# Four edits at the seams of a TensorE-bound kernel: weight rows and first tile in order of arrival, fold copies swapped between two engines, attention ahead of three output tiles, one output half moved to another engine

## Chip, cores and metric

One core of a Trainium2 chip. The metric is the device time of one execution in microseconds (us). Before the change: 220.64 us, median of 3 runs (220.44 to 220.81). Engines are called as the profile calls them: PE is TensorE, PEld its weight loads, DVE VectorE, ACT ScalarE, POOL GpSimd, SP the engine that here only starts DMAs. PE writes its results to banks of PSUM, from which DVE or ACT copies them before a bank is used again (here the first k tile waits 0.74 us for such a copy). The granted clock is the share of PE's full clock in the profile's records.

## The reference, cut to what matters

```python
def _A_ref(x, wqkv, w_phi, wo):          # linear attention, 32 heads of 16
    q, k, v = split(x @ wqkv)
    pq, pk = q @ w_phi, k @ w_phi        # per head
    phi = concat(softmax(p), softmax(-p))
    kv, z = phi_k^T v, sum(phi_k)
    return (phi_q kv / phi_q z) @ wo
def _B_ref(x, w_in, w_sp, b_sp, w_out):  # gated MLP, 688 + 688 columns
    z = gelu(x @ w_in); z1 = z[:688]; z2 = layernorm(z[688:])
    return (z1 * (w_sp @ z2 + b_sp)) @ w_out
out = g * A + (1 - g) * B                # g = sigmoid(x . gate_w), x is 2048 x 512
```

The kernel multiplies w_phi into wq and wk once ("folds"), so that pq and pk are single products with x.

## The kernel before

It has three stages: A, z tiles (z2 = second half of w_in, z1 = first half), with the folds between them; B, k, v and q tiles with exps and the kv sums; C, the product with w_sp ("gg"), attention tiles and output tiles. Cuts are marked `...`. `warm_up(n)` issues n matmuls on constants whose result nobody reads; they are called fillers below.

```python
def load_z2w(eng, j, h):                 # four pieces: column half j, d rows 2h and 2h+1
    eng.dma_start(out=w_z2[:, 2*h:2*h+2, j*HF:(j+1)*HF],
                  in_=w_in_v[:, 2*h:2*h+2, FH+j*HF:FH+(j+1)*HF])
nc.sync.dma_start(out=xs[:, 0, :], in_=x2[0:P, :])
load_z2w(nc.scalar, 0, 0); load_z2w(nc.sync, 0, 1); load_z2w(nc.scalar, 1, 0)
nc.sync.dma_start(out=xs[:, 1, :], in_=x2[P:2*P, :])
load_z2w(nc.sync, 1, 1)
nc.scalar.dma_start(out=xs[:, 2:4, :], ...)
...
def fold(qk, dt):
    ...                                  # four 128-column matmuls into one bank, fps
    if dt % 2 == 0: nc.scalar.copy(out=dst[:, dt, :], in_=fps[:, :])
    else:           nc.vector.tensor_copy(out=dst[:, dt, :], in_=fps[:, :])

warm_up(7); x_T(0); warm_up(5, P)        # x_T: transpose one x tile on PE
z_half(zps[0], 0, w_z2, 0, HF, lambda: x_T(1))   # tile 0, half 0; x tile 1 in the middle
gate_T(); warm_up(2, P)
z_half(zps[1], 1, w_z2, 0, HF); warm_up(2, P)
z_half(zps[0], 0, w_z2, 1, HF + 1); z2_tile(0, zps[0])
z_half(zps[1], 1, w_z2, 1, HF + 1, lambda: x_T(2)); z2_tile(1, zps[1])
x_T(3); z2_tile(2); z2_tile(3); b_T()    # b_T: one small transpose, used as a mark below
...
for hh in range(1, 2 * NT):              # stage C
    tt, j = divmod(hh, 2); gg_half(tt, j)
    if j == 1: uTs[tt] = u_T(tt)
    if j == 1 and tt >= 2: ba_tile(tt - 2, ...)          # output tile
    for k in attn_at.get(hh, ()): oTs[k] = attn_tile(k)  # tiles 0-4 at odd hh, 5-9 at even
ba_tile(NT - 2, ...); ba_tile(NT - 1, ..., nsplit=2)     # each half: ACT scales, ACT's queue stores
```

The softmax here doesn't subtract the row's maximum and nothing guards it: scores larger than these inputs give would overflow.

Of the kernel before, what the change touches and what calls it, by code (L numbers as in the profile page):

```python
# [7 lines left out]
AF = mybir.ActivationFunctionType  # L8
ALU = mybir.AluOpType
AX = mybir.AxisListType  # L10
FP32 = mybir.dt.float32
BF16 = mybir.dt.bfloat16
I32 = mybir.dt.int32

P = 128
# [4 lines left out]
F = 1376  # L20
FH = 688
HF = FH // 2
NT = S // P
NDT = D // P
CH = 512
# [9 lines left out]
def kernel(  # L35
# [14 lines left out]
    nc = tc.nc  # L50
    x2 = A_x.flatten_outer_dims()
    out2 = out.flatten_outer_dims()
# [5 lines left out]
    psF = psF_cm.__enter__()  # L58

    xT = pers.tile([P, NDT, S], BF16, name="xT")  # L60
    w_z1 = early.tile([P, NDT, FH], BF16, name="w_z1")
    w_z2 = early.tile([P, NDT, WP], BF16, name="w_z2")
# [24 lines left out]
    g_inv = pers.tile([P, NT], FP32, name="g_inv")  # L87
# [9 lines left out]
    w_in_v = B_w_in.rearrange("(dt p) f -> p dt f", p=P)  # L97
# [6 lines left out]
        out=ramp[:, 0, :], data0=ones32[:, :], data1=zeros[:, :], initial=0.0,  # L104
        op0=ALU.add, op1=ALU.add,
# [6 lines left out]
            out=ident[qs, qs], in0=ramp[qs, 0, :], in1=ramp[qs, 1, :], op=ALU.is_equal)  # L112
    nc.gpsimd.dma_start(out=gaterow[:, :], in_=gate_w.rearrange("(dt p) -> dt p", p=P))
    nc.gpsimd.dma_start(out=brow[:, :], in_=B_b_sp.rearrange("(t p) -> t p", p=P))
    def load_z2w(eng, j, h):
        eng.dma_start(
            out=w_z2[:, 2 * h:2 * h + 2, j * HF:(j + 1) * HF],
            in_=w_in_v[:, 2 * h:2 * h + 2, FH + j * HF:FH + (j + 1) * HF])

    nc.sync.dma_start(out=xs[:, 0, :], in_=x2[0:P, :])  # L120
    load_z2w(nc.scalar, 0, 0)
    load_z2w(nc.sync, 0, 1)
    load_z2w(nc.scalar, 1, 0)
    nc.sync.dma_start(out=xs[:, 1, :], in_=x2[P:2 * P, :])
    load_z2w(nc.sync, 1, 1)
    nc.scalar.dma_start(
        out=xs[:, 2:4, :], in_=x2[2 * P:4 * P, :].rearrange("(i p) d -> p i d", p=P))
    for h in range(2):
# [60 lines left out]
    psA_cm = tc.tile_pool(name="psA", bufs=3, space=bass.MemoryType.PSUM, reuse_waits="tile")  # L189
    psA = psA_cm.__enter__()  # L190

    def z_half(zp, tt, wt, j, n, mid=None):
        for dt in range(NDT):
            if dt == 2 and mid is not None:
                mid()
            nc.tensor.matmul(  # L196
                zp[:, j, 0:n], lhsT=xT[:, dt, tt * P:(tt + 1) * P],
                rhs=wt[:, dt, j * HF:j * HF + n],
                start=(dt == 0), stop=(dt == NDT - 1),
            )  # L200

    def z_mm(tt, wt, w):
        zp = psA.tile([P, 2, CH], FP32, name="zp")
        for dt in range(NDT):
            for j in range(2):
                n = HF if j == 0 else w - HF
                nc.tensor.matmul(  # L207
                    zp[:, j, 0:n], lhsT=xT[:, dt, tt * P:(tt + 1) * P],
                    rhs=wt[:, dt, j * HF:j * HF + n],
                    start=(dt == 0), stop=(dt == NDT - 1),  # L210
                )
        return zp

    def z2_tile(tt, zp=None):
        if zp is None:
            zp = z_mm(tt, w_z2, FH + 1)
        z2v = z2all[:, tt, :].rearrange("p (j n) -> p j n", j=2)
        nc.scalar.activation(out=z2v, in_=zp[:, :, 0:HF], func=AF.Gelu_apprx_tanh)  # L218
        nc.vector.tensor_copy(out=glog[:, tt:tt + 1], in_=zp[:, 1, HF:HF + 1])
        for j in range(2):  # L220
            nc.vector.bn_stats(out=bn6[:, tt, j, :], in_=z2v[:, j, :])  # L221
        nc.vector.bn_aggr(out=mv[:, tt, :], in_=bn6[:, tt, :, :].rearrange("p j s -> p (j s)"))
# [18 lines left out]
                op0=ALU.subtract, op1=ALU.mult,  # L241
            )

    wp = psF.tile([P, CH], FP32, name="wp", tag="pq", bufs=2)

    def warm_up(n, w=CH):
        for _ in range(n):
            nc.tensor.matmul(
                wp[:, 0:w], lhsT=nc.const_aps.tensor(1.0, [P, P], BF16),
                rhs=nc.const_aps.tensor(1.0, [P, w], BF16), start=True, stop=True)  # L250

    def x_T(i):
        tp = psF.tile([P, NDT, P], BF16, name="tp", tag="pq", bufs=2)
        for dt in range(NDT):
            nc.tensor.transpose(tp[:, dt, :], xs[:, i, dt * P:(dt + 1) * P], ident[:, :])
        with tc.high_priority():
            nc.vector.tensor_copy(out=xT[:, :, i * P:(i + 1) * P], in_=tp[:, :, :])  # L257

    def gate_T():
        gt = psF.tile([P, NDT], BF16, name="gt", tag="pq", bufs=2)  # L260
        nc.tensor.transpose(gt[:, :], gaterow[:, :], ident[0:NDT, 0:NDT])
        for dt in range(NDT):
            nc.vector.tensor_copy(out=w_z2[:, dt, FH:FH + 1], in_=gt[:, dt:dt + 1])
# [19 lines left out]
    def fold(qk, dt):  # L283
        dst = wq_p if qk == 0 else wk_p
        fps = psF.tile([P, CH], FP32, name="fps", tag="pq", bufs=2)
        for kc in range(NDT):
            nc.tensor.matmul(
                fps[:, kc * P:(kc + 1) * P],
                lhsT=wqkT[:, qk * 4 + kc, dt * P:(dt + 1) * P],
                rhs=wphi[:, kc, :],  # L290
                start=True, stop=True,
            )
        if dt % 2 == 0:
            nc.scalar.copy(out=dst[:, dt, :], in_=fps[:, :])
        else:
            nc.vector.tensor_copy(out=dst[:, dt, :], in_=fps[:, :])  # L296

    with tc.manual_schedule(engines={mybir.EngineType.PE, mybir.EngineType.Activation}):
        warm_up(7)
        x_T(0)  # L300
        warm_up(5, P)
        zps = [psA.tile([P, 2, CH], FP32, name="zp") for _ in range(2)]
        z_half(zps[0], 0, w_z2, 0, HF, lambda: x_T(1))
        gate_T()
        warm_up(2, P)
        z_half(zps[1], 1, w_z2, 0, HF)
        warm_up(2, P)
        z_half(zps[0], 0, w_z2, 1, HF + 1)
        z2_tile(0, zps[0])
        z_half(zps[1], 1, w_z2, 1, HF + 1, lambda: x_T(2))  # L310
        z2_tile(1, zps[1])
        x_T(3)
        z2_tile(2)
        z2_tile(3)
        b_T()
        for c in range(NCH):
            ts = list(range(c * 4, c * 4 + 4))
            for tt in ts:
                if c > 0:
                    z2_tile(tt)  # L320
                if c >= 2 and tt % 2 == 0:
                    fold(3 - c, (tt % 4) // 2)
            for tt in ts:
                z1_tile(tt)
                if c >= 2 and tt % 2 == 0:
                    fold(3 - c, 2 + (tt % 4) // 2)
            z2_norm(ts)
            if c == 1:
                wphi_fold()
# [144 lines left out]
    def ba_tile(tt, uT, oT, nsplit=1):  # L474
        w = D // nsplit
        for h in range(nsplit):
            acc = mm_tile()
            ba_mm(acc[:, 0:w], uT, oT, h * w, (h + 1) * w)
            ob = work.tile([P, w], BF16, name=f"ob{nsplit}")
            nc.scalar.activation(out=ob[:, :], in_=acc[:, 0:w], func=AF.Copy, scale=g_inv[:, tt:tt + 1])  # L480
            nc.scalar.dma_start(out=out2[tt * P:(tt + 1) * P, h * w:(h + 1) * w], in_=ob[:, :])

    oTs = {}
    uTs = {}
    with tc.manual_schedule(engines={mybir.EngineType.PE, mybir.EngineType.Activation}):
        ks = {0: k_tile(0)}
        kvacc = [psM.tile([P, NG, 256], FP32, name=f"kvacc{a}", tag="kvat", bufs=2) for a in range(2)]
        pend = []
        for tt in range(NT):
            if tt + 1 < NT:  # L490
                ks[tt + 1] = k_tile(tt + 1)
            ek, rk = ks.pop(tt)
            pend.append((tt, ek, v_tile(tt, rk)))
            pq_tile(tt // 4, tt % 4)
            if len(pend) > 2:
                kv_acc(*pend.pop(0))
        nc.scalar.activation(out=g_el[:, :], in_=glog[:, :], func=AF.Exp)
        nc.vector.tensor_scalar(out=g_1p[:, :], in0=g_el[:, :], scalar1=1.0, scalar2=None, op0=ALU.add)
        nc.vector.reciprocal(out=g_inv[:, :], in_=g_1p[:, :])
        kv_acc(*pend.pop(0))  # L500
        gg_half(0, 0)
        kv_acc(*pend.pop(0))
        kvz_evac()
        work_cm.__exit__(None, None, None)
        work = ctx.enter_context(tc.tile_pool(name="workC", bufs=2, reuse_waits="tile"))
        attn_at = {}
        for tt in range(NT):
            attn_at.setdefault(2 * tt + (1 if tt < 5 else 0 if tt < 10 else -1), []).append(tt)
        for hh in range(1, 2 * NT):
            tt, j = divmod(hh, 2)  # L510
            gg_half(tt, j)
            if j == 1:
                uTs[tt] = u_T(tt)
            if j == 1 and tt >= 2:
                ba_tile(tt - 2, uTs.pop(tt - 2), oTs.pop(tt - 2))
            for k in attn_at.get(hh, ()):
                oTs[k] = attn_tile(k)
        ba_tile(NT - 2, uTs.pop(NT - 2), oTs.pop(NT - 2))
        ba_tile(NT - 1, uTs.pop(NT - 1), oTs.pop(NT - 1), nsplit=2)


# [28 lines left out]
```

## Time and profile before

| reading | value | view |
|---|---|---|
| time | 220.64 us | median of 3 runs |
| PE busy | 211.7 of 219.0 us | page, part 1 |
| second x tile transposed from | 6.30 us | PE timeline |
| small bias transpose (end of the z2 tiles 0 to 3) | 12.36 us | PE timeline |
| first k tile | 48.30 us | timeline |

Head of the page before: the engine's busy time, share of the span and instructions.

```profile
span 219.0 us, 3717 instructions
## 1 busy us (share of the span) xinstructions
PE 211.7 (97%) x1436; PEld 130.6 (60%) x1456; DVE 148.8 (68%) x381; ACT 74.0 (34%) x120; POOL 13.8 (6%) x51
```

Only PE is near its span, and the change looks for its gain in PE's waits. The list of PE's waits before, beside 0.8 us at the launch (us in total, times, longest):

```profile
PE mm L346 <- DVE wq_p L296: 0.7, 1, 0.7
PE tp L255 <- DMA xs<-in_A_x_dram: 0.6, 1, 0.6
PE mm L363 <- ACT eq_686 L396: 0.3, 1, 0.3
PE gt L261 <- DVE xT L257: 0.2, 1, 0.2
PE at_1685 L431 <- DVE m L451: 0.2, 1, 0.2
```

There are five waits of 2 us in all, and they are what the change aims at. The PE timeline of the front (start, duration, line, output<-inputs, shape, count, idle time before):

```profile
4.92 0.75 PE L196 MATMUL zp<-w_z_66,xT 128*128 128x344 bf16 x2
6.30 0.40 PE L255 MATMUL tp<-ident,xs 128*128 128x128 bf16 x4 [0.63 <-DMA xs<-in_A_x_dram]
6.53 0.46 PE L196 MATMUL zp<-w_z_66,xT 128*128 128x344 bf16 x2
7.21 0.16 PE L261 MATMUL gt<-ident,gaterow 4*128 4x4 bf16 x1 [0.23 <-DVE xT L257]
...
9.91 2.51 PE L207 MATMUL zp<-w_z_66,xT 128*128 128x344 bf16 x16
12.36 0.18 PE L267 MATMUL bt<-ident,brow 16*128 16x16 bf16 x1
```

PE waits for the second x tile at 6.30 and has no gap after the third z2 tile at 9.91. The seam between stages A and B, in the timeline of all engines:

```profile
46.09 1.56 DVE L238 TENSOR_SCALAR z2all<-z2all,mv,rstd 128x688 bf16<-128x688 bf16 x4 [1.46 <-POOL rstd L236]
46.23 1.33 PE L207 MATMUL zp<-w_z_65,xT 128*128 128x344 bf16 x8
47.57 0.68 DVE L296 CAST wq_p<-fps 128x512 bf16<-128x512 f32 x1
48.30 1.02 PE L346 MATMUL mm<-wk_p,xT 128*128 128x512 bf16 x3 [0.74 <-DVE wq_p L296]
48.35 1.28 ACT L350 ACT_TABLE_LOAD   x1
```

The last fold's copy stands behind four norms on DVE, and the first k tile needs that bank. The attention tile that waits, in the PE timeline of stage C:

```profile
130.09 2.50 PE L415 MATMUL mm<-z2all,wspT 128*128 128x344 bf16 x16
132.56 0.42 PE L431 MATMUL at_1684<-kvz,eq_685 128*128 128x144 bf16 x4
133.16 0.42 PE L431 MATMUL at_1685<-kvz,eq_686 128*128 128x144 bf16 x4 [0.17 <-DVE m L451]
133.42 2.50 PE L415 MATMUL mm<-z2all,wspT 128*128 128x344 bf16 x16
```

### The profile page before, as it was taken

The page shows a single profiled execution, that of the slowest core. Times are in us where ns is not written, and L with a number is a line of the kernel's source. Part 1 is how long each engine was busy: PE and PEld are TensorE (multiplying, and loading weights), DVE is VectorE, ACT ScalarE, POOL GpSimd, SP SyncE. Part 2 cuts the span into 40 slices and gives each one's busy share as a digit, 9 for nine tenths or more (in the row PEclk, how much of TensorE's full clock was granted, in tenths as well). Part 3 has the DMA queues.
Part 4 walks back from the last instruction along what each step waited for, and adds up shares of the span by engine and source line. Part 5 has one row for each costly group of instructions (what it writes and reads, how often), then busy time and mean ns, then how long its engine had stood idle before and what let it go on. Part 6 is the DMA issues. An engine that isn't in the chain of part 4 may idle for free.

```text
span 219.0 us, 3717 instructions
## 1 busy us (share of the span) xinstructions
PE 211.7 (97%) x1436; PEld 130.6 (60%) x1456; DVE 148.8 (68%) x381; ACT 74.0 (34%) x120; POOL 13.8 (6%) x51
## 2 busy tenths in 40 slices
PE   8899999989999999999999999999999999999993
PEld 3566666754455555567756665656666666666653
DVE  3376776757999999985867659547648576458610
ACT  2256666678776767650001110110011001100112
POOL 7120202020000000000000000000000000000000
PEclk9999999999999999999999999999999999999998
DMA  6999999999940000000332331331343314312331
GB/s 193 258 215 198 247 260 210 251 266 265 192 148 0 3 0 0 3 3 0 63 63 57 87 61 47 84 63 38 71 87 61 77 40 77 84 36 59 77 84 49
DMA packets 71890, 22.30 MB, mean 102 GB/s; under 512 B 65936, under 2 KB 71872, under 8 KB 71872
## 3 DMA queue, kind: packets, MB, share of 16 engines
q1 hardware_dynamic: 68016, 19.33, 43.1%
q10 hardware_dynamic: 3792, 2.73, 4.2%
q8 instruction: 11, 0.18, 0.4%
q14 instruction: 7, 0.06, 0.1%
q0 software_dynamic: 64, 0.01, 0.0%
HBM read 3.71 MB, written 2.10 MB: 27 GB/s over the span
## 4 chain that ended last, share of the span: by engine, by line
PE 89%; DVE 4%; DMA 2%; ACT 2%; issue 1%; POOL 1%; SPq 0%
PE mm L415 33%; PE zp L207 13%; PE mm L472 9%; PE mm L363 6%; PE mm L391 6%; PE mm L470 6%; PE mm L346 6%; DMA xs<-in_A_x_dram 2%; PE kvacc_707 L381 2%; PE kvacc_708 L381 2%; DVE bn_83 L221 1%; PE zp L196 1%; DVE z2all L238 1%; DVE wq_p L296 1%; ACT eq_685 L396 1%
## 5 line engine op out<-in xcount | busy, mean ns | idle before, releaser
L415 PE MATMUL mm<-z2all,wspT 128*128 128x344 bf16 x512 | 78.3, 309 | 0.0
L415 PEld LDWEIGHTS <-wspT 128*128 128x128 bf16 x512 | 49.5, 98 | 23.4
L207 PEld LDWEIGHTS <-xT 128*128 128x128 bf16 x240 | 22.9, 98 | 10.8 <-DVE xT L257 0.2
L472 PE MATMUL mm<-w_out_t,uT 128*128 128x512 bf16 (+1 forms) x102 | 23.5, 366 | 0.0
L369 DVE TENSOR_TENSOR vr<-mm,rk 128x512 bf16<-128x512 f32 x32 | 21.2, 668 | 1.0 <-PE mm L363 0.9
L352 DVE TENSOR_REDUCE zk<-ek 128x64 f32<-128x1024 bf16 x16 | 19.3, 1211 | 3.4 <-ACT ek L350 3.4
L207 PE MATMUL zp<-w_z_65,xT 128*128 128x344 bf16 x128 | 20.0, 309 | 0.0
L350 ACT ACTIVATE ek<-mm 128x512 bf16<-128x512 f32 x32 | 17.3, 598 | 3.0 <-PE mm L346 2.8
L207 PE MATMUL zp<-w_z_66,xT 128*128 128x344 bf16 x112 | 17.7, 310 | 0.0
L363 PE MATMUL mm<-wv_sb,xT 128*128 128x512 bf16 x64 | 16.4, 379 | 0.4 <-ACT eq_686 L396 0.3
L346 PE MATMUL mm<-wk_p,xT 128*128 128x512 bf16 x60 | 15.9, 379 | 0.9 <-DVE wq_p L296 0.7
L470 PE MATMUL mm<-wo_t,oT 128*128 128x512 bf16 (+1 forms) x54 | 15.7, 363 | 0.7
L472 PEld LDWEIGHTS <-uT 128*128 128x128 bf16 x102 | 10.0, 98 | 10.8
L391 PE MATMUL mm<-xT,wq_p 128*128 128x512 bf16 x62 | 16.0, 379 | 0.0
L218 ACT ACTIVATE z2all<-zp 128x688 bf16<-128x688 f32 x16 | 11.9, 743 | 11.6 <-PE zp L207 6.7
L221 DVE BATCH_NORM_STATS2 bn_83<-z2all 128x6 f32<-128x344 bf16 x32 | 14.9, 502 | 0.0
L226 ACT ACTIVATE z1all<-zp 128x688 bf16<-128x688 f32 x16 | 11.9, 743 | 6.9 <-PE zp L207 6.9
L420 DVE SCALAR_TENSOR_TENSOR ucat_92<-mm,bT,z1all 128x344 bf16<-128x344 f32 x12 | 6.9, 572 | 9.9 <-PE mm L415 9.9
L396 ACT ACTIVATE eq_685<-mm 128x512 bf16<-128x512 f32 x16 | 9.6, 597 | 10.6 <-PE mm L391 9.3
L458 DVE TENSOR_TENSOR o<-m 128x512 bf16<-128x512 f32 x16 | 10.9, 680 | 0.0
L363 PEld LDWEIGHTS <-xT 128*128 128x128 bf16 x64 | 6.2, 98 | 7.8 <-issue 0.6
L391 PEld LDWEIGHTS <-wq_p 128*128 128x128 bf16 x64 | 6.3, 98 | 7.6
(221 smaller groups left out, 207.8 us busy)
## 6 DMA issues: line engine op xcount, KB each, us to landing
w_z_65<-in_B_w_in_dram SPq DMA_DIRECT2D x2, 344.0 KB, 5.2
w_out_t<-in_B_w_out_dram SPq DMA_DIRECT2D x1, 640.0 KB, 5.3
wv_sb<-in_A_wqkv_dram SPq DMA_DIRECT2D x1, 512.0 KB, 4.6
wo_t<-in_A_wo_dram SPq DMA_DIRECT2D x1, 512.0 KB, 5.7
w_z_66<-in_B_w_in_dram ACTq DMA_DIRECT2D x2, 172.0 KB, 3.3
w_z_66<-in_B_w_in_dram SPq DMA_DIRECT2D x2, 172.0 KB, 4.3
xs<-in_A_x_dram SPq DMA_DIRECT2D x2, 128.0 KB, 3.5
xs<-in_A_x_dram ACTq DMA_DIRECT2D x1, 256.0 KB, 5.3
```

The costliest lines, as they stand in the source:

```text
L207: nc.tensor.matmul(zp[:, j, 0:n], lhsT=xT[:, dt, tt * P:(tt + 1) * P], rhs=wt[:, dt, j * HF:j * HF + n], start=(dt == 0), stop=(dt == NDT ...
L218: nc.scalar.activation(out=z2v, in_=zp[:, :, 0:HF], func=AF.Gelu_apprx_tanh)
L221: nc.vector.bn_stats(out=bn6[:, tt, j, :], in_=z2v[:, j, :])
L346: nc.tensor.matmul(k_ps[:, :], lhsT=xT[:, dt, tt * P:(tt + 1) * P], rhs=wk_p[:, dt, :], start=(dt == 0), stop=(dt == NDT - 1))
L350: nc.scalar.activation(out=ek[:, a, :], in_=k_ps[:, :], func=AF.Exp, scale=1.0 - 2.0 * a)
L352: nc.vector.tensor_reduce(out=zk[:, :], in_=ek[:].rearrange("p a (h e) -> p (a h) e", e=DH), axis=AX.X, op=ALU.add,)
L363: nc.tensor.matmul(v_ps[:, :], lhsT=xT[:, dt, tt * P:(tt + 1) * P], rhs=wv_sb[:, dt, :], start=(dt == 0), stop=(dt == NDT - 1))
L369: nc.vector.tensor_tensor(out=vr[:, a, :, 0:P].rearrange("p g (h d) -> p g h d", d=DH), in0=v_ps[:, :].rearrange("p (g h d) -> p g h d", g ...
L391: nc.tensor.matmul(pq[:, :], lhsT=wq_p[:, dt, g * P:(g + 1) * P], rhs=xT[:, dt, c0:c0 + CH], start=(dt == 0), stop=(dt == NDT - 1),)
L415: nc.tensor.matmul(gp[:, 0:HF], lhsT=wspT[:, st, tt * P:(tt + 1) * P], rhs=z2all[:, st, j * HF:(j + 1) * HF], start=(st == 0), stop=(st == ...
L470: nc.tensor.matmul(acc, lhsT=oT[:, g, :], rhs=wo_t[:, g, c0:c1], start=(g == 0), stop=False)
L472: nc.tensor.matmul(acc, lhsT=uT[:, ft, :], rhs=w_out_t[:, ft, c0:c1], start=False, stop=(ft == NFT - 1))
```

## The change

Its intent: start the first tile with the rows that are there, take the last fold away from the busy DVE (the edit swaps the two engines for all eight folds), give DVE more time between two attention tiles, and free the tail from ACT. The diff, cut to its core and partly put in words:

```diff
-    load_z2w(nc.scalar, 0, 0) ... (nc.sync, 0, 1) ... (nc.scalar, 1, 0) ... (nc.sync, 1, 1)
+    def load_z2w(eng, dt):
+        eng.dma_start(out=w_z2[:, dt, 0:FH], in_=w_in_v[:, dt, FH:F])
+    load_z2w(nc.scalar, 0) ... (nc.sync, 1) ... (nc.scalar, 2) ... (nc.sync, 3)
 ...
-        z_half(...) gate_T() warm_up(2, P) z_half(...) ...      # as printed above
+        z2_tile(0, order=[(0,0),(1,0),(2,0),(0,1),(1,1),(2,1),(3,0),(3,1)],   # (d row, half)
+                mid={(2,0): [gate_T, lambda: x_T(1)], (2,1): [lambda: warm_up(4, P)]})
+        z2_tile(1, mid={(1,1): [lambda: x_T(2)], (2,1): [lambda: x_T(3)]})
 ...
-        if dt % 2 == 0:          # fold: ACT copies the even d blocks
+        if dt % 2 == 1:          # the last fold is dt = 3
 ...
-            ACT scales both halves of the last tile, ACT's queue stores them
+            if h == 0: as before
+            else: nc.vector.tensor_scalar(out=ob, in0=acc, scalar1=g_inv, op0=mult); nc.sync.dma_start(...)
 ...
-            if j == 1 and tt >= 2: ba_tile(tt - 2, ...)   # always ahead of attention
+            tt >= 5: ahead of attn_tile as before; tt = 2, 3, 4: after attn_tile
```

The warm-up matmuls also move from a bank of the transposes to a bank of the z tiles.

More of the change, by code (lines that the diff above doesn't have):

```diff
@@ L114 @@
     nc.gpsimd.dma_start(out=brow[:, :], in_=B_b_sp.rearrange("(t p) -> t p", p=P))
-    def load_z2w(eng, j, h):
-        eng.dma_start(
-            out=w_z2[:, 2 * h:2 * h + 2, j * HF:(j + 1) * HF],
-            in_=w_in_v[:, 2 * h:2 * h + 2, FH + j * HF:FH + (j + 1) * HF])
+    def load_z2w(eng, dt):
+        eng.dma_start(out=w_z2[:, dt, 0:FH], in_=w_in_v[:, dt, FH:F])
     nc.sync.dma_start(out=xs[:, 0, :], in_=x2[0:P, :])
-    load_z2w(nc.scalar, 0, 0)
-    load_z2w(nc.sync, 0, 1)
-    load_z2w(nc.scalar, 1, 0)
+    load_z2w(nc.scalar, 0)
+    load_z2w(nc.sync, 1)
+    load_z2w(nc.scalar, 2)
     nc.sync.dma_start(out=xs[:, 1, :], in_=x2[P:2 * P, :])
-    load_z2w(nc.sync, 1, 1)
+    load_z2w(nc.sync, 3)
     nc.scalar.dma_start(
@@ L190, with z_mm @@
     psA = psA_cm.__enter__()
-    def z_half(zp, tt, wt, j, n, mid=None):
-        for dt in range(NDT):
-            if dt == 2 and mid is not None:
-                mid()
+    def z_mm(tt, wt, w, order=None, mid={}):
+        zp = psA.tile([P, 2, CH], FP32, name="zp")
+        for dt, j in order or [(dt, j) for dt in range(NDT) for j in range(2)]:
+            n = HF if j == 0 else w - HF
             nc.tensor.matmul(
@@ L200, in z_half, with z2_tile @@
             )
-    def z_mm(tt, wt, w):
-        zp = psA.tile([P, 2, CH], FP32, name="zp")
-        for dt in range(NDT):
-            for j in range(2):
-                n = HF if j == 0 else w - HF
-                nc.tensor.matmul(
-                    zp[:, j, 0:n], lhsT=xT[:, dt, tt * P:(tt + 1) * P],
-                    rhs=wt[:, dt, j * HF:j * HF + n],
-                    start=(dt == 0), stop=(dt == NDT - 1),
-                )
-        return zp
-    def z2_tile(tt, zp=None):
-        if zp is None:
-            zp = z_mm(tt, w_z2, FH + 1)
+            for f in mid.get((dt, j), ()):
+                f()
+        return zp
+    def z2_tile(tt, **kw):
+        zp = z_mm(tt, w_z2, FH + 1, **kw)
         z2v = z2all[:, tt, :].rearrange("p (j n) -> p j n", j=2)
@@ L242, in z2_norm @@
             )
-    wp = psF.tile([P, CH], FP32, name="wp", tag="pq", bufs=2)
+    wp = psA.tile([P, 2, CH], FP32, name="zp")
     def warm_up(n, w=CH):
@@ L248, in warm_up @@
             nc.tensor.matmul(
-                wp[:, 0:w], lhsT=nc.const_aps.tensor(1.0, [P, P], BF16),
+                wp[:, 0, 0:w], lhsT=nc.const_aps.tensor(1.0, [P, P], BF16),
                 rhs=nc.const_aps.tensor(1.0, [P, w], BF16), start=True, stop=True)
@@ L301 @@
         warm_up(5, P)
-        zps = [psA.tile([P, 2, CH], FP32, name="zp") for _ in range(2)]
-        z_half(zps[0], 0, w_z2, 0, HF, lambda: x_T(1))
-        gate_T()
-        warm_up(2, P)
-        z_half(zps[1], 1, w_z2, 0, HF)
-        warm_up(2, P)
-        z_half(zps[0], 0, w_z2, 1, HF + 1)
-        z2_tile(0, zps[0])
-        z_half(zps[1], 1, w_z2, 1, HF + 1, lambda: x_T(2))
-        z2_tile(1, zps[1])
-        x_T(3)
+        z2_tile(
+            0, order=[(0, 0), (1, 0), (2, 0), (0, 1), (1, 1), (2, 1), (3, 0), (3, 1)],
+            mid={(2, 0): [gate_T, lambda: x_T(1)], (2, 1): [lambda: warm_up(4, P)]},
+        )
+        z2_tile(1, mid={(1, 1): [lambda: x_T(2)], (2, 1): [lambda: x_T(3)]})
         z2_tile(2)
@@ L479, in ba_tile @@
             ob = work.tile([P, w], BF16, name=f"ob{nsplit}")
-            nc.scalar.activation(out=ob[:, :], in_=acc[:, 0:w], func=AF.Copy, scale=g_inv[:, tt:tt + 1])
-            nc.scalar.dma_start(out=out2[tt * P:(tt + 1) * P, h * w:(h + 1) * w], in_=ob[:, :])
+            dst = out2[tt * P:(tt + 1) * P, h * w:(h + 1) * w]
+            if h == 0:
+                nc.scalar.activation(out=ob[:, :], in_=acc[:, 0:w], func=AF.Copy, scale=g_inv[:, tt:tt + 1])
+                nc.scalar.dma_start(out=dst, in_=ob[:, :])
+            else:
+                nc.vector.tensor_scalar(
+                    out=ob[:, :], in0=acc[:, 0:w], scalar1=g_inv[:, tt:tt + 1], scalar2=None, op0=ALU.mult)
+                nc.sync.dma_start(out=dst, in_=ob[:, :])
     oTs = {}
@@ L513 @@
                 uTs[tt] = u_T(tt)
-            if j == 1 and tt >= 2:
+            ba = j == 1 and tt >= 2
+            if ba and tt >= 5:
                 ba_tile(tt - 2, uTs.pop(tt - 2), oTs.pop(tt - 2))
@@ L517 @@
                 oTs[k] = attn_tile(k)
+            if ba and tt < 5:
+                ba_tile(tt - 2, uTs.pop(tt - 2), oTs.pop(tt - 2))
         ba_tile(NT - 2, uTs.pop(NT - 2), oTs.pop(NT - 2))
```

## The prediction

> **What bounds it now.** TensorE. The page's busy table gives PE 211.7 of 219.0 us (97%); the chain that ended last is 89% PE. By timeline and waits only these places can pay:
>
> 1. Front. PE idles from 5.67 to 6.30 us until the second x tile lands (6.25), 0.2 us more before the gate transpose (7.21), and 0.17 us before the third z2 tile, which starts at 9.91. Then PE is back to back.
> 2. Fold. The last wq fold leaves PSUM on DVE only after four norms (46.09-47.65; copy 47.57-48.25). The first k tile needs that bank: PE ends its last z1 tile at about 47.4 and starts k at 48.30.
> 3. PE waits 0.2 us at attention tile 5: VectorE still reads the previous banks.
> 4. Tail: ACT evacuates the last half tile in 0.47 us.
>
> **What the change does, with its cost.**
>
> (1) The 688 KB of gate-half weights come in rows of 1376 bytes instead of 688. [...] The first tile can use three d rows before x tile 1 arrives, which pulls one 0.145 us matmul into the gap; the gate transpose no longer waits for a copy; two more matmuls cover the third x transpose. But the fourth row is the last load on its queue, where the present last piece lands at 7.7 us. PE will stall for it (to 7.4-7.6), then needs about 1.9 us (10 matmuls, two transposes) before the third z2 tile: start near 9.45 instead of 9.91. Gain 0.45 us (0.2 to 0.8).
>
> (2) ACT takes the last fold behind the Gelu that starts at 46.21: copy about 46.85-47.43, k near 47.5, 0.8 us earlier. Exp still starts at 49.64: it waits for the last Gelu and a 1.28 us table load. PE runs ahead on four banks and ACT loses its present idle 0.24 and 0.53 us, so about 0.7 survives to the third v tile (now 55.68). VectorE needs 2.73 us a tile against PE's 3.06 and does not take it back.
>
> (3) Attention before the output matmuls for tiles 2 to 4 puts 1.9 us more between attention tiles 4 and 5: the wait vanishes, 0.2 us.
>
> (4) VectorE evacuates 256 columns in an estimated 0.41 us (0.68 for 512, 0.18 for 32): 0.06 us.
>
> Sum 0.45+0.7+0.2+0.06 = 1.4 us, all on the critical path: 220.64 - 1.4 = 219.2 us, range 218.5 to 219.9. Faster by over 2%: 0.02; within 2%: 0.97; slower: 0.01.
>
> **What would show it.** Third z2 tile at 9.1-9.7 after a PE wait on the fourth weight row; the k tile's DVE wait gone, and first k tile 0.8 us nearer to the third z2 tile; waits on exp among the first k/v tiles; no wait at attention tile 5; a DVE operation of about 0.4 us at the end.
>
> **What would make it wrong.** The fourth row landing after 8 us eats (1). A delayed last Gelu delays the exps, eating (2). [...]

## The result, and the profile after

219.39 us (median of 4 runs, 219.04 to 219.40) against 220.54 (4 runs of before beside it): ratio 0.9942, 95% interval 0.9925 to 0.9960. A ratio here is the mean time of one kernel's fast runs over the mean of the other's of the same rounds, so it is not quite the ratio of the medians. The gain is about half a per cent, with an interval clear of 1. Over all that was run later the changed kernel has a median of 219.40 us (16 runs) and before 220.47 (48 runs), which is 1.07 us less.

The page after:

```profile
span 217.0 us, 3736 instructions
...
PE 212.6 (98%) x1456; PEld 130.9 (60%) x1456; DVE 149.6 (69%) x382; ACT 73.5 (34%) x119; POOL 13.8 (6%) x51
```

PE's waits after, beside the one for the launch:

```profile
PE mm L345 <- ACT eq_686 L378: 0.2, 1, 0.2
```

Four of the five waits are gone, and the one on exp stays. The PE timeline of the front after:

```profile
4.92 1.04 PE L194 MATMUL zp<-w_z_66,xT 128*128 128x344 bf16 x3
5.90 0.18 PE L249 MATMUL gt<-ident,gaterow 4*128 4x4 bf16 x1
6.01 0.61 PE L243 MATMUL tp<-ident,xs 128*128 128x128 bf16 x4
6.41 0.75 PE L194 MATMUL zp<-w_z_66,xT 128*128 128x345 bf16 x3
7.00 0.39 PE L236 MATMUL zp<-const-bfloat16-1.0 128*128 128x128 bf16 x4
7.23 1.04 PE L194 MATMUL zp<-w_z_66,xT 128*128 128x344 bf16 x6
11.57 0.18 PE L255 MATMUL bt<-ident,brow 16*128 16x16 bf16 x1
```

Here the second x tile is used at 6.01, the fourth weight row at 7.23 (it landed at about 7.18), and the bias transpose comes 0.79 us earlier than before. The seam between A and B after:

```profile
45.45 1.33 PE L194 MATMUL zp<-w_z_65,xT 128*128 128x344 bf16 x8
45.65 1.57 DVE L226 TENSOR_SCALAR z2all<-z2all,mv,rstd 128x688 bf16<-128x688 bf16 x4 [1.46 <-POOL rstd L224]
46.07 0.58 ACT L282 CAST wq_p<-fps 128x512 bf16<-128x512 f32 x1
46.70 1.89 PE L328 MATMUL mm<-wk_p,xT 128*128 128x512 bf16 x8
47.57 1.28 ACT L332 ACT_TABLE_LOAD   x1
```

ACT copies the fold while DVE does the norms. From the start of the last z1 tile to the first k tile it is 1.25 us (46.70 - 45.45) where it was 2.07 (48.30 - 46.23). Attention tile 5 after:

```profile
128.56 2.50 PE L397 MATMUL mm<-z2all,wspT 128*128 128x344 bf16 x16
130.90 0.41 PE L413 MATMUL at_1684<-kvz,eq_685 128*128 128x144 bf16 x4
131.15 0.41 PE L413 MATMUL at_1685<-kvz,eq_686 128*128 128x144 bf16 x4
131.40 2.50 PE L397 MATMUL mm<-z2all,wspT 128*128 128x344 bf16 x16
```

From gg to gg the stretch takes 2.84 us (131.40 - 128.56); before it was 3.33 (133.42 - 130.09). The last evacuation, before on ACT and after on DVE:

```profile
215.71 0.47 ACT L480 ACTIVATE ob_2607<-mm,g_inv 128x256 bf16<-128x256 f32 x1 [0.61 <-PE mm L472]
```

```profile
213.68 0.48 DVE L467 TENSOR_SCALAR ob_2607<-mm,g_inv 128x256 bf16<-128x256 f32 x1 [5.92 <-PE mm L454]
```

0.47 against 0.48 us: no gain.

One warning lies in these two profiles. Their spans differ by 2.0 us, but the times differ by 1.15. The profiled run of before (220.96 us) was slower than all four runs timed beside it, and that of after (219.04) was the fastest of its four. So a part read from one pair of traces can be chance. The experiments had to say which part.

### The profile page after: what moved, and what is told of

It reads as the page before. It is cut to its first block, busy times and chain, and to the rows that moved or that the text cites. A ratio compares the mean times of both kernels' runs of the same rounds, so it can differ in the third digit from the quotient of the medians.

```text
span 217.0 us, 3736 instructions
## 1 busy us (share of the span) xinstructions
PE 212.6 (98%) x1456; PEld 130.9 (60%) x1456; DVE 149.6 (69%) x382; ACT 73.5 (34%) x119; POOL 13.8 (6%) x51
## 4 chain that ended last, share of the span: by engine, by line
PE 98%; ACT 1%; DVE 0%; issue 0%
PE mm L397 34%; PE zp L194 18%; PE mm L454 10%; PE mm L345 6%; PE mm L373 6%; PE mm L452 6%; PE mm L328 6%; PE zp L236 2%; PE kvacc_708 L363 2%; PE kvacc_707 L363 2%; PE fps L275 1%; PE tp L243 1%; ACT eq_685 L378 0%; ACT eq_686 L378 0%; DVE ob_2607 L467 0%; PE wps L261 0%
## 5 line engine op out<-in xcount | busy, mean ns | idle before, releaser
L194 PEld LDWEIGHTS <-xT 128*128 128x128 bf16 x256 | 24.4, 98 | 11.5 <-DVE xT L245 0.2
L194 PE MATMUL zp<-w_z_66,xT 128*128 128x344 bf16 (+1 forms) x128 | 21.3, 315 | 0.0
L194 PE MATMUL zp<-w_z_65,xT 128*128 128x344 bf16 x128 | 20.0, 309 | 0.0
L452 PE MATMUL mm<-wo_t,oT 128*128 128x512 bf16 (+1 forms) x68 | 16.6, 367 | 0.0
L206 ACT ACTIVATE z2all<-zp 128x688 bf16<-128x688 f32 x16 | 11.9, 743 | 10.9 <-PE zp L194 10.9
L402 DVE SCALAR_TENSOR_TENSOR ucat_92<-mm,bT,z1all 128x344 bf16<-128x344 f32 x12 | 6.9, 573 | 12.2 <-PE mm L397 12.2
L214 ACT ACTIVATE z1all<-zp 128x688 bf16<-128x688 f32 x16 | 11.9, 743 | 6.9 <-PE zp L194 6.9
L402 DVE SCALAR_TENSOR_TENSOR ucat_93<-mm,bT,z1all 128x344 bf16<-128x344 f32 x10 | 5.7, 572 | 7.6 <-PE mm L397 7.6
```

The lines of the kernel that those rows point to most:

```text
L194: nc.tensor.matmul(zp[:, j, 0:n], lhsT=xT[:, dt, tt * P:(tt + 1) * P], rhs=wt[:, dt, j * HF:j * HF + n], start=(dt == 0), stop=(dt == NDT ...
L402: nc.vector.scalar_tensor_tensor(out=ucat[tt % NU][:, j * HF:(j + 1) * HF], in0=gp[:, 0:HF], scalar=bT[:, tt:tt + 1], in1=z1all[:, tt, j * ...
L452: nc.tensor.matmul(acc, lhsT=oT[:, g, :], rhs=wo_t[:, g, c0:c1], start=(g == 0), stop=False)
```

## The experiments

Kernels are compared only within the same rounds. Times are medians. All gave a correct result. For the parts, each profile is cut at four marks on PE: the bias transpose, the third v tile, attention tile 6, and the last output matmul group.

| profile | bias transpose at | to third v tile | to attention tile 6 | to last output group | from there to the end of the span |
|---|---|---|---|---|---|
| before | 12.36 | 43.32 | 84.57 | 74.60 | 4.15 |
| after | 11.57 | 42.58 | 84.07 | 74.60 | 4.18 |
| front_only | 12.09 | 43.32 | 84.56 | 74.61 | 4.12 |
| fold_only | 11.76 | 42.58 | 84.57 | 74.61 | 4.08 |
| attn_only | 12.10 | 43.32 | 84.07 | 74.60 | 4.11 |
| tail_only | 11.98 | 43.32 | 84.57 | 74.60 | 4.13 |
| all_but_front | 12.06 | 42.58 | 84.07 | 74.60 | 4.09 |
| after_again | 11.44 | 42.58 | 84.07 | 74.60 | 4.11 |
| after_third | 12.06 | 42.58 | 84.07 | 74.60 | 4.19 |

### One part alone: four kernels

**front_only.** The kernel before with the first two hunks of the diff (loads, order) and the warm-up's bank, nothing else.

> The kernel before with only the front changed (row loads, order of arrival, warm-up bank). Prediction on record: 0.45 us faster than before. Theory T (distances between matching PE starts in the two traces): 0.77 us faster, third z2 tile near 9.14 us instead of 9.91. Rival S (timed total of 1.15 us is the truth, so one part gives less than its trace shows, and the front is the part that hangs on landings[...]): 0.0 to 0.4 us. Expected time by T about 219.8, by S about 220.3.

Measured: 220.82 us against 220.63 beside it, ratio 1.0021 (0.9967 to 1.0076). Six runs: 219.68, 220.51, 220.63, 221.02, 222.82, 222.90. The two last had a mean granted clock of 0.992. In its profile PE waited 1.1 us for the second x tile (line below), and the bias transpose came at 12.09, not 11.6. Theory T, which took 0.77 us from the pair of traces, falls. The lower end of theory S, no gain, fits, and the two runs at low clock were expected by nobody.

```profile
6.73 0.40 PE L243 MATMUL tp<-ident,xs 128*128 128x128 bf16 x4 [1.09 <-DMA xs<-in_A_x_dram]
```

**fold_only.**

```diff
-        if dt % 2 == 0:
+        if dt % 2 == 1:
             nc.scalar.copy(out=dst[:, dt, :], in_=fps[:, :])
```

> The kernel before with only the fold's evacuation moved (odd d blocks on ACT). Prediction on record: 0.7 us. T: 0.8 us earlier at the first k tile, of which 0.74 us is left at the third v tile and after; time about 219.85. S allows the same here. Rival: if ACT delayed the last Gelu and so the exps, under 0.3 us.

Measured: 219.62 against 220.63, ratio 0.9942 (0.9911 to 0.9974). In the table it takes 0.74 us (43.32 - 42.58) in every profile that has it, and touches nothing else. The median moved by 1.0, more than the cut; medians of six runs scatter by a few tenths.

**attn_only.**

```diff
-            if j == 1 and tt >= 2: ba_tile(...)
-            for k in ...: attn_tile(k)
+            ba = j == 1 and tt >= 2
+            if ba and tt >= 5: ba_tile(...)
+            for k in ...: attn_tile(k)
+            if ba and tt < 5: ba_tile(...)
```

> The kernel before with only the order of attention and output matmuls for tiles 2 to 4 changed. Prediction on record: 0.2 us, the idle time that the list of waits shows. T (start to start, 132.42 expected against 133.42 less 0.51 of its own work): 0.49 us. Time by T about 220.1, by the record 220.35.

Measured: 220.00 against 220.63, ratio 0.9958 (0.9927 to 0.9989). The table says 0.50 us (84.57 - 84.07), as T had it and not the 0.2 of the record.

**tail_only.** Only the hunk with `nc.vector.tensor_scalar` and `nc.sync.dma_start`.

> The kernel before with only the last half output tile on VectorE and the SP queue. Prediction on record: 0.06 us. T: 0.0 us (0.48 us on DVE against 0.47 on ACT, issue to landing alike). Both inside the noise of about 0.1 to 0.2 us; over 0.3 us either way refutes both.

Measured: 220.73 against 220.63, ratio 0.9994 (0.9963 to 1.0025): nothing, as the last column says.

### What is the front worth?

**all_but_front.** The changed kernel with the loads and PE order of before.

> The changed kernel with the front of before put back (piece loads, old order). The five profiles so far add up as fold 0.74 us (bias transpose to third v tile 43.32 against 42.58), attention 0.50 us (third v tile to attention tile 6: 84.57 against 84.07), tail 0.0. Theory U: these two carry all of the change that is certain, so 1.24 us faster than before, about 219.35, with the bias transpose of the front anywhere between 11.7 and 12.4 us. Rival T (front worth 0.77 us of its own): this kernel would have to be 0.7 us slower than the changed one run beside it.

Measured: 219.43 against 220.53, ratio 0.9968 (0.9939 to 0.9997; one run of 221.5 is in the mean). **after_again**:

> The changed kernel once more. U: its front hangs on one landing, bias transpose about 4.39 us after the fourth weight row lands (11.57 for 7.18, 12.09 for 7.7 in the two profiles of the new front). Time within 0.4 us of the kernel with the old front, 219.0 to 219.6. T: 218.7.

Measured: 219.30 (the same runs of before), ratio 0.9963 (0.9932 to 0.9993), five runs of 218.93 to 219.62 and one of 221.48 at clock 0.992. So with and without the front the kernels are 0.13 us apart by the medians; U holds, T does not. In all four profiles of the new front the bias transpose comes exactly 4.34 us after the matmul on the fourth row starts (7.23, 7.75, 7.10, 7.72), and that row had just landed (at about 7.2, 7.7, 7.1 and 7.7). It is not the only landing that holds the front: the second x tile was used at 6.01, 6.73, 5.75 and 6.56, and behind it PE still had a transpose, three matmuls and four fillers to do. With 0.23 us for the fillers (7.00 to 7.23 in the first), PE waited for the row an estimated 0.00, 0.12, 0.44 and 0.26 us beyond that work; an earlier row alone could have gained no more. In the five profiles of the old front the second x tile was transposed at 5.48 to 6.30 us, and the mark came 6.06 to 6.28 us after that.

**rows_old_order** and **pieces_new_order** take the loads and the order apart.

```diff
 # rows_old_order: all_but_front, with
-load_z2w(eng, j, h), four pieces
+load_z2w(eng, dt), four rows
 # pieces_new_order: the changed kernel, with
-load_z2w(eng, dt), four rows
+load_z2w(eng, j, h), four pieces
```

> Row loads with the old PE order. The first tile's first half then needs the fourth row, which lands at 7.2 to 7.7 us, before anything else may go on: bias transpose about 5.5 us later, at 12.7 to 13.2, so 0.7 us slower than the kernel with the old front. [...] Shows that rows without the new order lose.

Measured: profile with the fourth row used at 7.00 after a wait of 0.73 us and the bias transpose at 12.39, better than the 12.7 to 13.2 expected from a row that lands at 7.2 to 7.7. But the time was 221.78 us, ratio 1.0043 (1.0002 to 1.0083): two runs of 219.8 to 219.9, and four of 221.6 to 222.9, these four at clock 0.990 to 0.992.

> The new PE order with the old 688-byte pieces. The sixth matmul needs the last piece (7.0 to 7.7 us in the four profiles of the old loads), bias transpose about 4.75 us after it, 11.75 to 12.45; 0.3 us slower than the changed kernel for equal landings. [...]

Measured: 219.63, ratio 0.9967 (0.9954 to 0.9980), bias transpose at 11.99, with a wait of 0.94 us for the last piece, used at 7.26. That is what was expected for equal landings. Rows were not seen to land earlier than pieces: the last row landed at 7.0 to 7.7 us in the profiles, the last piece at 7.0 to 7.7 too. A scatter of 0.7 us would hide a difference of a few tenths.

### The runs at low clock

Four runs of 22 with the new front (front_only and three times the changed kernel) had a mean clock near 0.992 and took 221.5 to 222.9 us. None of 68 runs with the old front had (44 of before, with a clock on record, and 24 of kernels with its front). They count as fast, since they are less than 1.5% above the fastest. rows_old_order had them in four of six. Two kernels ask whether PE's idle time in the front causes them.

```diff
 # rows_old_fill: rows_old_order, with 14 filler matmuls ahead of the fourth row's first matmul
+            if dt == 3 and fill: warm_up(fill, P)      # fill=14 for tile 0, half 0
 # rows_old_nofill: rows_old_order, without the fillers of the front
-        warm_up(5, P)
-        warm_up(2, P)      # twice
```

> Row loads, old order, with 14 idle-work matmuls of 128 columns put into the stall for the fourth row (0.73 us in the profile without them). In the kernel without them 4 of 6 runs had a mean granted clock of 0.990 to 0.992 and were 2 us slower. Theory V: the clock falls to half for one stretch after the stall (0.8 per cent of 219 us at half speed costs about 1.7 us), so with the stall filled no or one run of 6 is at 0.992 and the median goes from 221.8 to about 219.9. Rival W: those runs are slow for a reason outside the kernel (the run, the chip): 4 of 6 stay slow, median near 221.8.

Measured: 220.47 against 220.39, ratio 0.9996 (0.9983 to 1.0009), none of five runs at low clock (0.998 to 1.0). The slow runs went, as V says. The median missed the 219.9: in its profile the loads were late (the second x tile used at 6.30) and the fillers lasted until the fourth row's matmul at 7.61.

> The same kernel with the nine short filler matmuls of the front taken out as well. V: TensorE rests longer before and after the stall, so 4 to 6 of 6 runs at 0.992 or less[...], median at or over 221.8[...]. W: no more slow runs than in other kernels, time up to 0.4 us shorter for the matmuls left out.

Measured: 220.83, ratio 1.0012 (0.9984 to 1.0039), three of six runs at 0.991 or 0.992, on the same chip in which the filled kernel had none and before had none in 11. Three is fewer than the 4 to 6 expected, and the median is under 221.8; but W, by which the chip makes them, falls. The counts are small, and the fillers seem to have a price: the three runs without them at full clock took 219.54 to 220.53 us, the five with them 220.03 to 220.59. The profile fell in a run at low clock. Its table by stretches (from:to, length, PE, PEld, DVE, ACT, POOL busy, then granted clock, DMA share, GB/s):

```profile
core 0: us, PE busy (x) PEld busy (x) DVE busy (x) ACT busy (x) POOL busy (x), PEclk, DMA share, GB/s
5.00:6.00 1.00, 0.49 (x2) 0.05 (x2) 0.00 (x0) 0.00 (x0) 0.94 (x8) 1.00 1.20 324
6.00:7.00 1.00, 0.54 (x5) 0.34 (x6) 0.22 (x1) 0.00 (x0) 0.22 (x2) 1.00 1.04 239
7.00:8.00 1.00, 0.31 (x2) 0.08 (x1) 0.21 (x1) 0.00 (x0) 0.00 (x0) 1.00 1.07 367
8.00:9.00 1.00, 1.00 (x7) 0.62 (x8) 0.36 (x4) 0.00 (x0) 0.00 (x0) 0.79 2.18 193
9.00:10.00 1.00, 1.00 (x5) 0.55 (x4) 0.00 (x0) 0.00 (x0) 0.00 (x0) 0.50 0.78 155
10.00:11.00 1.00, 1.00 (x8) 0.72 (x6) 0.00 (x0) 0.74 (x1) 0.00 (x0) 0.50 1.20 232
11.00:12.00 1.00, 1.00 (x8) 0.73 (x6) 0.42 (x1) 0.36 (x1) 0.00 (x0) 0.51 0.59 126
12.00:13.00 1.00, 1.00 (x9) 0.66 (x7) 0.91 (x3) 0.38 (x1) 0.00 (x0) 1.00 1.24 275
```

The same stretches of the filled kernel, cut:

```profile
6.00:7.00 1.00, 0.70 (x11) 0.66 (x12) 0.27 (x1) 0.00 (x0) 0.22 (x2) 1.00 1.13 253
7.00:8.00 1.00, 1.00 (x15) 0.69 (x13) 0.16 (x1) 0.00 (x0) 0.00 (x0) 1.00 1.05 354
...
9.00:10.00 1.00, 1.00 (x11) 0.73 (x10) 0.00 (x0) 0.44 (x1) 0.00 (x0) 1.00 1.11 228
```

In the kernel without fillers PE is 31 to 54% busy from 5 to 8 us (and 48% from 4 to 5). Then, with work at hand again, the granted clock is 0.50 from about 8.57 to 11.99 us (the stretch 8.5:8.7 has a mean of 0.69, 11.9:12.0 one of 0.56) and 1.00 after that. In the filled kernel PE is 94, 70 and 100% busy in the slices from 5 to 8 us, and the clock stays at 1.00 up to 14 us, where the table ends. That is one profile of each kernel: what makes the clock fall, and why it does so only in some runs, is not shown. By an estimate from these figures, half speed for 3.42 us (11.99 - 8.57) costs about 1.7 us, and 1.7 of 219.7 is the 0.8% by which the mean clock of such runs falls. The slow runs of the changed kernel have the same mean clock (0.991 and 0.992), but none of them was profiled, so whether they had such a stretch, and where, is open.

### A version meant to beat both

**swap_fill.** If one landing holds the front, load that row sooner, and put the fillers where PE waits anyway.

```diff
-    load_z2w(nc.sync, 3)
-    nc.scalar.dma_start(out=xs[:, 2:4, :], ...)
+    load_z2w(nc.scalar, 3)
+    nc.sync.dma_start(out=xs[:, 2:4, :], ...)
-                mid={(2,0): [gate_T, lambda: x_T(1)], (2,1): [lambda: warm_up(4, P)]})
+                mid={(2,0): [gate_T, lambda: warm_up(4, P), lambda: x_T(1)]})
```

> A version of the changed kernel meant to beat both: the fourth weight row goes third on the ACT queue and the x tiles 2 and 3 last on the SP queue, and the four fillers stand before the transpose of x tile 1 in place of before the fourth row. If the front hangs on the landing of the fourth row (U), it lands by about 6.5 us instead of 7.1 to 7.7, bias transpose at 11.0 to 11.4 instead of 11.4 to 12.1, median about 218.9, and fewer slow runs. If all loads of the front land together whatever their order, bias transpose stays near 11.5 and the time near 219.3.

Measured: 218.91 us against 220.39, ratio 0.9922 (0.9909 to 0.9935). All six runs lie between 218.19 and 219.01, none at low clock. The row landed at about 7.0 us, not 6.5, and the bias transpose came at 11.36. So the size of the gain came as expected, but less by an earlier landing than thought. The swap and the moved fillers were not run apart, and the changed kernel was not in this call; its ratios to before were 0.9942, 0.9963 and 0.9981. The interval of swap_fill lies wholly below that of the last of these three and overlaps the other two (from 0.9925 and 0.9932), so that it beats the changed kernel is likely, but not shown. By the medians it gains 1.48 us on the runs beside it, where the changed kernel gains 1.07 over all its runs.

**after_third.** The changed kernel once more, to count.

> The changed kernel a third time, for its front and its slow runs. So far the new front left the bias transpose at 11.57, 12.09 and 11.44 us (mean 11.70), the old one at 12.36, 11.76, 12.10, 11.98 and 12.06 (mean 12.05); so 0.35 us less, with a spread as large. U and V together: bias transpose at 11.4 to 12.1, most runs 219.0 to 219.6, ratio to before 0.994 to 0.995 without slow runs, 0 to 2 of 6 runs at a clock of 0.992 and 221 to 222 us. If the front is worth the 0.77 us of T after all: under 219.0 in most runs.

Measured: 219.68 against 220.32, ratio 0.9981 (0.9946 to 1.0016). Four runs of 219.20 to 219.82, one of 221.64 at clock 0.991, and one of 223.15 at clock 1.0. Bias transpose at 12.06. The run of 223.15 is marked slow (over 1.5% above the fastest) and is not in the ratio; the median of the other five is 219.53. The run of 221.64 takes about half of the gain out of the mean.

## Why the prediction was right or wrong

The total was right: 219.2 predicted, 219.39 measured, inside the range. The gain was 1.15 us in the first four runs and 1.07 over all, for 1.4 predicted. The terms were not all right: attention was forecast 0.3 us too low, front and tail together 0.25 us or more too high. That the total came out so close was in part luck.

1. *Fold, 0.7 us: right, with its mechanism.* k came 0.82 us nearer (2.07 - 1.25, predicted 0.8), PE ran ahead while ACT still loaded its table (1.28 us), the wait on exp stayed, and 0.74 us was left at the third v tile and after. DVE did not take it back: the next two columns of the table do not move.
2. *Attention, 0.2 us: mechanism right, the term mis-sized; it was 0.50.* "PE waits 0.2 us at attention tile 5" took the list's idle time. That list counts idle time behind the modelled end of the last matmul, and it saw only the second half of the tile. Start to start the trace of before already had it: four attention matmuls take 0.25 us without a wait (130.90 to 131.15 and on to 131.40 in the profile after), and here the first group began 0.14 us late (132.56 against 130.09 + 2.33) and the two groups took 0.86 instead of 0.50, together 0.50.
3. *Front, 0.45 us (0.2 to 0.8): mis-sized; it is about 0.3 by the mark and about none by the medians.* The mark stood at 12.05 us on average in five profiles of the old front and at 11.79 in four of the new, each scattering by 0.6. Medians with and without the front differ by 0.13 us. The predicted start of the third z2 tile with the new front, 9.45, was good: it stands 2.43 us ahead of the mark (9.14 against 11.57 in the first), at 9.01 to 9.66 in the four profiles, 9.36 on average. The step that failed is the base: "which starts at 9.91" and the x tile "lands (6.25)" came from one profile, the latest of five, whose second x tile was 0.4 to 0.8 us later than the others'. That longer rows land sooner was not seen (the last load landed at 7.0 to 7.7 us with rows and with pieces). That PE "will stall" for the fourth row was right in kind in three of the four profiles (0.12 to 0.44 us). In the first of them the fillers covered the wait.
4. *Tail, 0.06 us: it was 0.* The 256 columns took 0.48 us on DVE, not 0.41.
5. *The runs at low clock: without a number in the forecast.* 4 of 22 runs with the new front had a mean clock near 0.992 and were about 2 us longer each. A clock of 0.50 is seen in one profile in the front, that of rows_old_nofill (8.57 to 11.99 us, with PE 31 to 54% busy from 5 to 8). The forecast's sentence on the clock is cut, and none of its terms allowed for such runs.

Open: the cuts of the profiles add up to more (0.74 + 0.50 + 0.26 = 1.50) than the medians show (1.07); the front's share, the only one that varies from run to run, is the likely place, but only the profiled runs can be cut. Open too: why loads of the same size land up to 0.8 us apart from run to run, and the four slow runs without a low mean clock (222.15 and 222.31 of before, 223.15 of the changed kernel, 221.50 of all_but_front), none of which was the profiled one. For these there is a candidate that no run tests. The granted clock reads 1.00 from 0 to 5 us in the profiles before and after, but in both the first seven fillers of 512 columns took 0.42 us each (from 0.83 to 3.77 us), and the k matmuls of as many columns 0.215 (46.70 to 48.42 in the profile after). The next five of 128 columns took 0.74 us in the profile after and 0.45 in after_again (4.20 to 4.94, 4.02 to 4.47), so how long this lasts differs between runs of one kernel. The mean clock of the profile after is 1.000 all the same: slow work at the start doesn't show in it, and a run with more of such work would be longer without a lower mean clock.

## What to carry to other kernels

Size a wait by the distance between the starts of the work on both sides of it, held against a place where the same work runs without the wait, and cut several profiles at the same marks before you believe a gain at a place that hangs on DMA landings. In a kernel like this one, try filler work where PE must wait for loads in its first microseconds: here the wait itself cost tenths (0.73 us in rows_old_order), and the runs at low clock, four of six of that kernel and none of five with the wait filled, took about 2 us more. Count several runs with and without, since the fillers take time too. When small edits are bundled, run each alone: here two carried 1.24 us, one nothing, and one, the front, gained little if anything and brought slow runs with it.
